# A planner that knows that two vector engines take turns, and that picks the engine itself

## Chip, cores and metric

The kernel runs on 1 core of one Trainium2 chip. The metric is device time in microseconds (us) of one execution; lower is better. The kernel before was run three times: 959.18, 959.60 and 962.43 us, median 959.6. TensorE (PE) multiplies matrices, VectorE (DVE) and GpSimd (POOL) do arithmetic on tiles, ScalarE (ACT) copies, rounds and applies functions, and SyncE (SP) issues the DMAs. SBUF is the working memory, PSUM the memory that matmuls write, in 8 banks.

## What is computed

```python
x = attention(q, k, v)      # 4 batches, 8 heads, 576 tokens, head size 64; 4 heads local, 4 strided
x = x / sqrt(mean(x*x) + 1e-6) * rms_g          # 2304 tokens x 512
x = (silu(x @ w_gate) * (x @ w_val)) @ w_out    # d_ff 1536
out = softplus(x @ w_in) @ w_out2               # d_ff 2048
```

The result is compared in float32. The weights are float64 on the host; the kernel gets their 64-bit words and decodes them to float32 on ACT and DVE.

## The kernel before

A float32 product is made of three matmuls in a reduced 32-bit format: every operand is split into a high half `h` (an ACT copy that rounds) and a low half `l = x - h` (a two-tile subtraction), and h·h, h·l and l·h are added in PSUM (`mm3`, L343 is the matmul). So each operand tile costs one ACT copy and one subtraction: `split_op` for the activations (tiles `ob`, `tb`), `part` in `prep_in` for the first weights (`win`), `prep_out` for the second weights (`wout`), `halves` for the hidden activations (`gh`/`gl`, `ghx`/`glx`).

The work runs in three stages, each recorded first and then emitted. Stage 1 is attention for batches 0 and 1. Stage 2 is attention for batches 2 and 3, laid between the first gated layer's products for tokens 0 to 1023 (`side_a`). Stage 3 holds the rest: the end of that half, `combine` and `build` (sums and differences of activation blocks for a seven-product block multiplication, `quad`), the gated layer for tokens 1024 to 2303 (f = 0 to 11), and the second layer for both halves (p = 0 to 7 twice). `out1` and `out2` multiply by the second weights; their results are added from a PSUM bank into `xs` on DVE (L771 for `out1`, L789 for `out2`), and the bank is free for the next product only after that. `plus` (L690) adds a PSUM bank to a tile in the same way, and L738 multiplies gate and value.

No instruction is placed by hand. Every step goes through `Program.add`, with its engine, an assumed duration, and the tiles that it reads and writes. `Program.emit` then plays the work through: it takes the engine that can start earliest, and of that engine's ready instructions the one with the smallest due time, counted back from the fixed order of the matmuls. The order of starts so found is the order in which each engine's instructions are issued. Engines take their instructions strictly in that order on the chip. Before, each step has a fixed engine, named in the code, and all engines are assumed to run independently. The function `two` (a two-tile sum, difference or product) goes to DVE or POOL as its caller says, with an assumed 110 + n/0.96 ns on DVE and 110 + 2.5n ns on POOL for n elements per partition:

```python
    def two(eng, n, name, o, x, y, r, w):
        if eng == "DVE":
            dve(n, lambda: getattr(nc.vector, name)(o, x, y), r, w)
        else:
            pool(n, lambda: getattr(nc.gpsimd, name)(o, x, y), r, w)
```

In the trace L263 is this operation on DVE and L265 the same on POOL. L280, L282 and L285 are the three DVE steps of `decode`. L361 to L364 are `stats` (1/rms), whose matmul with ones is L357.

Of the kernel before, what the change touches and what calls it, by code (L numbers as in the profile page):

```python
# [46 lines left out]
HOP = {"PE": 210, "DVE": 135, "ACT": 150, "POOL": 90, "SP": 60}  # L47


class Program:  # L50

    def __init__(self):
        self.nodes, self.seen, self.ends = [], {}, []
        self.free = dict.fromkeys(HOP, 0.0)
        self.side = False
        self.landed = 0.0

    def add(self, eng, dur, fn, r=(), w=(), kb=0):
        i = len(self.nodes)
        deps = set()
        for (key, lo, hi), wr in [(x, False) for x in r] + [(x, True) for x in w]:
            old = self.seen.setdefault(key, [])
            keep = []
            for e in old:
                if e[0] < hi and lo < e[1]:
                    if wr or e[3]:
                        deps.add(e[2])  # L70
                    if wr and lo <= e[0] and e[1] <= hi:
                        continue
                keep.append(e)
            keep.append((lo, hi, i, wr))
            self.seen[key] = keep
        deps.discard(i)
        self.nodes.append((eng, dur, fn, deps, 5 * kb, self.side))

    def emit(self, start=5000):
        nodes, n0, n = self.nodes, len(self.ends), len(self.nodes)  # L80
        new = range(n0, n)
        succ = {i: [] for i in new}
        left = dict.fromkeys(new, 0)
        ready = dict.fromkeys(new, 0.0)
        begin = {}

        def hop(d, i):
            e = nodes[d][0]
            return 0 if e == "PE" == nodes[i][0] else HOP[e]

        for i in new:
            for d in nodes[i][3]:
                if d < n0:
                    ready[i] = max(ready[i], self.ends[d] + hop(d, i))
                else:
                    left[i] += 1
                    succ[d].append(i)
        due = {}
        t = max(start, self.free["PE"])
        for i in new:  # L100
            due[i] = 1e12
            if nodes[i][0] == "PE":
                due[i] = t
                t += nodes[i][1]
        for i in reversed(new):
            for j in succ[i]:
                due[i] = min(due[i], due[j] - nodes[i][1] - nodes[i][4] * 2 - HOP[nodes[i][0]])
        streams = [[i for i in new if nodes[i][0] == "PE" and nodes[i][5] == s] for s in (False, True)]
        heads = [0, 0]
        free = self.free  # L110
        wait = {e: [] for e in HOP}
        avail = {e: [] for e in HOP}

        def release(i):
            if nodes[i][0] != "PE":
                heapq.heappush(wait[nodes[i][0]], (ready[i], i))

        for i in new:
            if not left[i]:
                release(i)  # L120
        ends = {}
        while len(ends) < len(new):
            best = None
            for e in HOP:
                at, s = None, 0
                if e == "PE":
                    for x in (0, 1):
                        if heads[x] < len(streams[x]) and not left[streams[x][heads[x]]]:
                            b = max(free[e], ready[streams[x][heads[x]]])
                            if at is None or b < at:  # L130
                                at, s = b, x
                elif avail[e]:
                    at = free[e]
                elif wait[e]:
                    at = max(free[e], wait[e][0][0])
                if at is not None and (best is None or at < best[0]):
                    best = (at, e, s)
            at, e, s = best
            if e == "PE":
                i = streams[s][heads[s]]  # L140
                heads[s] += 1
            else:
                while wait[e] and wait[e][0][0] <= at:
                    _, i = heapq.heappop(wait[e])
                    heapq.heappush(avail[e], (due[i], i))
                _, i = heapq.heappop(avail[e])
            begin[i] = at
            free[e] = at + nodes[i][1]
            ends[i] = free[e]
            if e == "SP":  # L150
                self.landed = max(self.landed, at + 400) + nodes[i][4]
                ends[i] = self.landed + 1100
            for j in succ[i]:
                ready[j] = max(ready[j], ends[i] + hop(i, j))
                left[j] -= 1
                if not left[j]:
                    release(j)
        for i in sorted(new, key=lambda i: (begin[i], i)):
            nodes[i][2]()
        self.ends += [ends[i] for i in new]  # L160
# [3 lines left out]
def attn_glu_softplus(  # L164
# [27 lines left out]
    def pool(n, fn, r, w):  # L192
        pr.add("POOL", 110 + n * 2.5, fn, r, w)

    def dma(kb, fn, r, w):
        pr.add("SP", 650, fn, r, w, kb=kb)
# [62 lines left out]
        sub(eng, n, l, src, h.bitcast(F32), [ksrc, kh], [kl])  # L259

    def two(eng, n, name, o, x, y, r, w):
        if eng == "DVE":
            dve(n, lambda: getattr(nc.vector, name)(o, x, y), r, w)  # L263
        else:
            pool(n, lambda: getattr(nc.gpsimd, name)(o, x, y), r, w)  # L265

    def sub(eng, n, o, x, y, r, w):
        two(eng, n, "tensor_sub", o, x, y, r, w)
# [557 lines left out]
    def w_at(f, side):  # L826
        return (f % 2, 0) if side else (0, f % 2 * 4)
# [12 lines left out]
    def prep2(p, all4, eng):  # L840
        i = ((W1N + p) % 2, 0)
        o = 3 * W1N + 4 * p
        prep_in(i, [(o, None), (o + 2, None)], True, all4, eng)
        for j in (0, 1):
            prep_out((2 * p + j) % 4, o + 2 * j + 1, None)
        return i

    with tc.manual_schedule():
# [140 lines left out]
        for side, (c0, c1, c4) in enumerate(SIDES):  # L989
# [3 lines left out]
            for p in range(n2):  # L993
                i = prep2(p, c4 is not None, "POOL" if p == 0 or side == 0 and p < 4 else "DVE")
# [85 lines left out]
```

## Time and profile before

| | |
|---|---|
| runs, median (lowest to highest) | 959.6 us (959.18 to 962.43) |
| the profiled execution | 961.84 us |
| its span, first to last instruction | 959.9 us |
| mean granted TensorE clock | 0.987 |
| PE busy | 906.0 us (94%) |
| DVE busy | 725.6 us (76%), 1184 instructions |
| ACT busy | 488.9 us (51%) |
| POOL busy | 229.8 us (24%), 201 instructions |

Busy is time in which an instruction of the engine was in execution. Two neighbours on DVE may overlap a little at their ends; the overlap counts once. The granted clock is the share of TensorE's full speed that was granted: 1.00 is 2.4 GHz, 0.5 is 1.2 GHz.

### The profile page before, as it was taken

The page shows a single profiled execution, that of the slowest core. Times are in us where ns is not written, and L with a number is a line of the kernel's source. Part 1 is how long each engine was busy: PE and PEld are TensorE (multiplying, and loading weights), DVE is VectorE, ACT ScalarE, POOL GpSimd, SP SyncE. Part 2 cuts the span into 40 slices and gives each one's busy share as a digit, 9 for nine tenths or more (in the row PEclk, how much of TensorE's full clock was granted, in tenths as well). Part 3 has the DMA queues.
Part 4 walks back from the last instruction along what each step waited for, and adds up shares of the span by engine and source line. Part 5 has one row for each costly group of instructions (what it writes and reads, how often), then busy time and mean ns, then how long its engine had stood idle before and what let it go on. Part 6 is the DMA issues. An engine that isn't in the chain of part 4 may idle for free.

```text
span 959.9 us, 14020 instructions
## 1 busy us (share of the span) xinstructions
PE 906.0 (94%) x5244; PEld 742.4 (77%) x5244; DVE 725.6 (76%) x1184; ACT 488.9 (51%) x917; POOL 229.8 (24%) x201
## 2 busy tenths in 40 slices
PE   6877999999997899999999988999989999999998
PEld 5655778778876788888788766888877888888886
DVE  6688778899389885889887796687689647666654
ACT  4677665646355465544444546655454564443331
POOL 2463102232048452324223372100023000000000
PEclk9999999999999899999999998999999999999999
DMA  9937676743140442344453013531211411101002
GB/s 193 212 116 205 178 240 176 227 149 130 66 132 22 143 118 91 99 132 145 163 174 100 23 44 100 163 89 56 76 33 39 138 43 35 44 26 42 22 1 110
DMA packets 42035, 103.11 MB, mean 107 GB/s; under 512 B 5040, under 2 KB 5744, under 8 KB 41968
## 3 DMA queue, kind: packets, MB, share of 16 engines
q1 hardware_dynamic: 41968, 102.23, 35.9%
q8 instruction: 41, 0.67, 0.3%
q14 instruction: 26, 0.21, 0.1%
HBM read 79.66 MB, written 22.54 MB: 106 GB/s over the span
## 4 chain that ended last, share of the span: by engine, by line
PE 70%; DVE 19%; DMA 4%; issue 3%; ACT 3%; POOL 1%; SPq 0%; DVEq 0%; ACTq 0%
PE bank L343 65%; DVE w L263 3%; PE bank L451 2%; DVE xs L771 2%; DVE cvu L282 2%; PE bank L532 2%; DVE cvu L280 1%; PE bank L508 1%; DMA w<-w_kept 1%; DMA id_sb<-ident 1%; DVE xs L263 1%; DVE wout L263 1%; DVE win L263 1%; DVE tb L263 1%; DVE gv L690 1%
## 5 line engine op out<-in xcount | busy, mean ns | idle before, releaser
L343 PE MATMUL bank<-ob,win 128*128 128x512 f32 (+1 forms) x1560 | 336.9, 362 | 12.0 <-ACT ob L258 3.8
L343 PEld LDWEIGHTS bank<-ob,win 128*128 128x128 f32 x1560 | 265.2, 190 | 64.2 <-ACT win L314 4.6
L343 PE MATMUL bank<-tb,win 128*128 128x512 f32 x672 | 175.5, 397 | 12.0 <-ACT ssq L686 5.5
L343 PEld LDWEIGHTS bank<-tb,win 128*128 128x128 f32 x672 | 125.9, 191 | 41.7 <-ACT ssq L686 7.4
L314 ACT ACTIVATE win<-w 128x512 fp32r<-128x512 f32 (+1 forms) x136 | 82.8, 615 | 92.2 <-DVE w L263 34.6
L789 DVE TENSOR_TENSOR xs<-bank,xs 128x512 f32<-128x512 f32 x126 | 86.7, 689 | 49.2 <-PE bank L343 48.6
L263 DVE TENSOR_TENSOR win<-w,win 128x512 fp32r<-128x512 f32 x102 | 72.7, 714 | 29.1 <-ACT win L314 28.8
L343 PE MATMUL bank<-wout,ghx 128*128 128x512 f32 x304 | 94.1, 391 | 0.4 <-DVE xs L789 0.3
L343 PE MATMUL bank<-gh,wout 128*128 128x512 f32 (+1 forms) x256 | 83.1, 361 | 7.4 <-DVE xs L771 5.9
L343 PE MATMUL bank<-ghx,wout 128*128 128x512 f32 x224 | 86.2, 404 | 0.2 <-DVE xs L771 0.2
L265 POOL TENSOR_TENSOR win<-w,win 128x512 fp32r<-128x512 f32 x34 | 49.2, 1449 | 155.1 <-ACT win L314 143.5
L343 PE MATMUL bank<-wout,gh 128*128 128x512 f32 x272 | 83.8, 390 | 0.0
L771 DVE TENSOR_TENSOR xs<-bank,xs 128x512 f32<-128x512 f32 (+1 forms) x100 | 62.2, 630 | 15.0 <-PE bank L343 14.2
L263 DVE TENSOR_TENSOR w<-w 128x256 f32<-128x256 f32 x112 | 71.9, 642 | 1.4
L343 PEld LDWEIGHTS bank<-wout,ghx 128*128 128x128 f32 x304 | 56.6, 188 | 12.9 <-DVE xs L789 1.6
L343 PEld LDWEIGHTS bank<-gh,wout 128*128 128x128 f32 x256 | 46.4, 192 | 16.9 <-DVE xs L771 7.9
L343 PE MATMUL bank<-wout,glx 128*128 128x512 f32 x152 | 59.3, 390 | 0.3 <-DVE glx L263 0.3
L343 PEld LDWEIGHTS bank<-wout,gh 128*128 128x128 f32 x272 | 50.9, 188 | 10.5
L343 PE MATMUL bank<-wout,gl 128*128 128x512 f32 x136 | 52.9, 389 | 0.0
L282 DVE SCALAR_TENSOR_TENSOR cvu<-raw,cvu 128x512 uint32<-128x512 uint32 x68 | 51.7, 760 | 1.4
L265 POOL TENSOR_TENSOR gl<-ssq,gh 128x256 fp32r<-128x256 f32 (+1 forms) x21 | 22.3, 1064 | 120.1 <-ACT gh L726 120.1
L726 ACT ACTIVATE gh<-ssq 128x512 fp32r<-128x512 f32 (+1 forms) x41 | 23.0, 564 | 54.2 <-PE bank L343 37.1
(157 smaller groups left out, 1412.8 us busy)
## 6 DMA issues: line engine op xcount, KB each, us to landing
raw<-w SPq DMA_DIRECT2D x68, 512.0 KB, 4.2
w<-w_kept SPq DMA_DIRECT2D x56, 256.0 KB, 2.7
w_kept<-cvtx SPq DMA_DIRECT2D x26, 256.0 KB, 4.2
cvt<-w_kept SPq DMA_DIRECT2D x26, 256.0 KB, 3.0
w_kept<-w SPq DMA_DIRECT2D x24, 256.0 KB, 3.9
w_kept<-cvt SPq DMA_DIRECT2D x18, 256.0 KB, 3.8
cvtx<-w_kept SPq DMA_DIRECT2D x18, 256.0 KB, 2.7
out<-xs SPq DMA_DIRECT2D x18, 256.0 KB, 2.0
```

Of the source, the lines that this page charges most:

```text
L263: dve(n, lambda: getattr(nc.vector, name)(o, x, y), r, w)
L265: pool(n, lambda: getattr(nc.gpsimd, name)(o, x, y), r, w)
L280: dve(512, lambda: nc.vector.tensor_scalar(out=u, in0=t.bitcast(U32), scalar1=0x80000000, scalar2=None, op0=ALU.bitwise_and), [kt], [ku], ...
L282: dve(512, lambda: nc.vector.scalar_tensor_tensor(out=u, in0=wlo, scalar=29, in1=u, op0=ALU.logical_shift_right, op1=ALU.bitwise_or), [kra ...
L314: act(n, lambda: nc.scalar.activation(h, t, AF.Copy), [kt], [reg(0, o + lo, o + hi)])
L343: lambda a=a, b=b, i=i, st=st, mv=mv: nc.tensor.matmul(o, lhsT=st[a], rhs=mv[b], start=(first and i == 0), stop=(last and i == m - 1), ski ...
L451: pr.add("PE", 108 if loc else 81, lambda a=a, h=h: nc.tensor.matmul(sp[64 * h:64 * h + 64, a * nk:(a + 1) * nk], lhsT=qt[:, h, q0 + a * s ...
L508: pr.add("PE", 109, lambda a=a, a0=a0, tp=tp: nc.tensor.transpose(tp[:kp, a * 128:a * 128 + 128], pv[:, a0 + a, :], id_sb), [kpv, all_of(" ...
L532: pr.add("PE", 81, lambda a=a, h=h, o=o, t=t: nc.tensor.matmul(xb[64 * h:64 * h + 64, a * nq:(a + 1) * nq], lhsT=vt[r0:r1, v0 + a, 64 * h: ...
L726: act(n, lambda: nc.scalar.activation(h, src, AF.Copy), [ksrc], [kh])
L771: dve(n, lambda: nc.vector.tensor_add(x, pb, x), [kp, kx], [kx])
L789: dve(DM, lambda: nc.vector.tensor_add(x, pb, x), [kp, kx], [kx])
```

## The change

It changes the planner and `two`, and no tile, matmul or transfer.

First, a step is marked as one that uses the port when it is on DVE or POOL and none of its tiles is a PSUM bank. The planner lets such steps run only one at a time, whichever of the two engines they are on (`self.port`). DVE has two queues for this: `DVE0` for steps with a bank, which start whenever DVE is free, and `DVE1` for the others.

Second, `two` ignores the engine that its caller names. The step is recorded for DVE with an alternative for POOL. In planning it stands in the queues `DVE1` and `FLEX`; POOL takes it from `FLEX` only if DVE has 900 ns or more of bank work before it (`BESIDE`). Its assumed durations become 60 + n/0.96 ns on DVE and 110 + 2.3n ns on POOL.

```diff
+BESIDE = 900
...
+        port = eng in ("DVE", "POOL") and not any("bank" in x[0] for x in [*r, *w])
...
+            return ("DVE1", "FLEX") if alt else (f"DVE{int(nodes[i][6])}",)
...
+            t0, t1 = earliest("DVE0", free["DVE"]), earliest("DVE1", max(free["DVE"], self.port))
...
+            base = max(free["POOL"], self.port)
+            t = earliest("FLEX", base)
+            if t is not None:
+                beside = max(0, free["DVE"] - t) + sum(nodes[i][1] for _, i in avail["DVE0"])
+                if beside >= BESIDE:
+                    offer(t, "POOL", "FLEX")
+            offer(earliest("POOL", base), "POOL", "POOL")
...
+                if s == "FLEX":
+                    nodes[i] = ("POOL", nodes[i][7][0], nodes[i][7][1]) + nodes[i][3:]
...
+            if nodes[i][6]:
+                self.port = free[e]
...
     def two(eng, n, name, o, x, y, r, w):
-        if eng == "DVE":
-            dve(n, lambda: getattr(nc.vector, name)(o, x, y), r, w)
-        else:
-            pool(n, lambda: getattr(nc.gpsimd, name)(o, x, y), r, w)
+        pr.add("DVE", 60 + n / 0.96, lambda: getattr(nc.vector, name)(o, x, y), r, w,
+               alt=(110 + n * 2.3, lambda: getattr(nc.gpsimd, name)(o, x, y)))
```

Counted over the whole program, 118 steps of `two` go from POOL to DVE and 7 the other way, so DVE has 111 instructions more and POOL 111 fewer. 2 of the 118 are in stage 1, 6 in stage 2 and 110 in stage 3. POOL keeps what attention gives it, and 9 steps of `two`. In stage 3 the matmuls stand in the same order as before.

The lines move by 39 or 40: before's L263 is L303 after (L304 on POOL), L771 is L810, L738 is L777, L690 is L729, L343 is L382, L357 is L396.

DVE, early in stage 3, while the last `out1` of tokens 0 to 1023 runs beside `combine` and `build` (win: first weights, wout: second weights, w32: weights being prepared; the last row before is the addition at 311.45 us in the trace). Before:

```order
L263 TENSOR_TENSOR ssq_65<-xs_64 128x512
L771 TENSOR_TENSOR xs_64<-bank3_74,xs_64 128x512
L263 TENSOR_TENSOR w32_83<-w32_83 128x256
L263 TENSOR_TENSOR gv0_84<-xs_64,ssq_65 128x512
L263 TENSOR_TENSOR tb_2521<-ssq_65,tb_2521 128x512
L263 TENSOR_TENSOR ob_67<-xs_64,ob_67 128x512 x2
L263 TENSOR_TENSOR tb_2521<-gv0_84,tb_2521 128x512
L263 TENSOR_TENSOR wout0_91<-cvt0_81,wout0_91 128x512
L263 TENSOR_TENSOR wout1_860<-cvtx_869,wout1_860 128x512
L738 TENSOR_TENSOR ssq_65<-bank6_77,ssq_65 128x512
L771 TENSOR_TENSOR xs_64<-bank4_75,xs_64 128x512
```

Now, from the same first row to the same last row:

```order
L303 TENSOR_TENSOR ssq_65<-xs_64 128x512
L303 TENSOR_TENSOR w32_83<-w32_83 128x256
L303 TENSOR_TENSOR ob_67<-xs_64,ob_67 128x512
L303 TENSOR_TENSOR tb_2521<-gv0_84,tb_2521 128x512
L303 TENSOR_TENSOR w32_83<-w32_83 128x256
L303 TENSOR_TENSOR tb_2521<-ssq_65,tb_2521 128x512
L303 TENSOR_TENSOR gv0_84<-xs_64,ssq_65 128x512
L303 TENSOR_TENSOR w32_83<-w32_83 128x256
L777 TENSOR_TENSOR ssq_65<-bank6_77,ssq_65 128x512
L303 TENSOR_TENSOR win0_90<-w32_83,win0_90 128x512
L303 TENSOR_TENSOR ob_67<-xs_64,ob_67 128x512
L810 TENSOR_TENSOR xs_64<-bank4_75,xs_64 128x512
```

The two `wout` subtractions and two of the `ob` and `tb` ones now stand behind the addition from the bank; a `win` subtraction that was POOL's stands ahead of it.

DVE, at the end of the gated layer, where `build` makes the operands of the second layer. Before:

```order
L690 TENSOR_TENSOR gv0_84<-bank3_74,gv0_84 128x512
L263 TENSOR_TENSOR w32_83<-w32_83 128x256
L280 TENSOR_SCALAR cvu0_82<-cvt0_81 128x512
L263 TENSOR_TENSOR w32_83<-w32_83 128x256
L282 SCALAR_TENSOR_TENSOR cvu0_82<-raw0_79,cvu0_82 128x512
L738 TENSOR_TENSOR gv0_84<-gv1_85,gv0_84 128x512
L263 TENSOR_TENSOR ssq_65<-xs_64 128x512
L771 TENSOR_TENSOR xs_64<-bank4_75,xs_64 128x512
L263 TENSOR_TENSOR w32_83<-w32_83 128x256
L285 SCALAR_TENSOR_TENSOR cvt0_81<-cvt0_81,cvu0_82 128x512
L771 TENSOR_TENSOR xs_64<-bank5_76,xs_64 128x512
```

Now:

```order
L729 TENSOR_TENSOR gv0_84<-bank3_74,gv0_84 128x512
L303 TENSOR_TENSOR ob_67<-xs_64,ob_67 128x512
L303 TENSOR_TENSOR gl1_89<-ssq_65,gh1_87 128x512
L303 TENSOR_TENSOR ob_67<-xs_64,ob_67 128x512
L777 TENSOR_TENSOR gv0_84<-gv1_85,gv0_84 128x512
L810 TENSOR_TENSOR xs_64<-bank4_75,xs_64 128x512
L303 TENSOR_TENSOR ssq_65<-xs_64 128x512
L810 TENSOR_TENSOR xs_64<-bank5_76,xs_64 128x512
L303 TENSOR_TENSOR glx0_866<-gv0_84,ghx0_863 128x512
```

The preparation of later weights (`w32`, `cvu`, `cvt`) has gone back, and the low halves `gl` and `glx`, which were POOL's, stand among the additions.

PE, from the end of stage 1 into stage 2. L532 (L571 after) is attention's last product, L343 (L382) the first gated layer's, L357 (L396) the matmul of `stats` for tokens 512 to 1023. Before:

```order
L532 MATMUL bank5_76<-pt2_117,vb1_106 64x54 x6
L532 MATMUL bank5_76<-pt3_118,vb1_106 64x54 x4
L343 MATMUL bank7_78<-ob_67,win0_90 128x512 x3
L343 MATMUL bank6_77<-ob_67,win0_90 128x512 x12
L357 MATMUL bank2_73<-ssq_65,ones_61 128x512
L343 MATMUL bank0_71<-ob_67,win0_90 128x512 x12
```

Now:

```order
L382 MATMUL bank7_78<-ob_67,win0_90 128x512 x12
L382 MATMUL bank6_77<-ob_67,win0_90 128x512 x6
L571 MATMUL bank5_76<-pt2_117,vb1_106 64x54 x6
L571 MATMUL bank5_76<-pt3_118,vb1_106 64x54 x4
L382 MATMUL bank6_77<-ob_67,win0_90 128x512 x6
L382 MATMUL bank0_71<-ob_67,win0_90 128x512 x12
L396 MATMUL bank2_73<-ssq_65,ones_61 128x512
```

The `stats` matmul now stands behind the 12 matmuls of bank0. The first 9 matmuls of bank7, which were spread among attention's before, now stand together near its end.

## Rows read from the trace of the kernel before

**Rows 1.** The page: busy time, share of the span and instructions by engine.

```profile
PE 906.0 (94%) x5244; PEld 742.4 (77%) x5244; DVE 725.6 (76%) x1184; ACT 488.9 (51%) x917; POOL 229.8 (24%) x201
```

**Rows 2.** Busy time by stretch: length, PE, PEld, DVE, ACT, POOL, clock, DMA share, GB/s.

```profile
276.00:325.00 49.00, 41.02 (x166) 31.80 (x165) 48.28 (x59) 23.85 (x45) 37.02 (x27) 0.95 0.22 68
325.00:345.00 20.00, 19.53 (x99) 16.56 (x98) 15.50 (x22) 11.02 (x21) 7.30 (x6) 0.94 0.44 138
345.00:545.00 200.00, 195.83 (x1025) 167.15 (x1024) 159.86 (x242) 95.91 (x176) 63.71 (x50) 1.00 0.39 124
545.00:600.00 55.00, 47.07 (x196) 36.63 (x195) 46.00 (x66) 30.73 (x56) 26.48 (x19) 0.91 0.21 63
...
705.00:740.00 35.00, 30.54 (x128) 23.38 (x127) 34.60 (x47) 20.39 (x37) 15.73 (x10) 1.00 0.11 31
```

**Rows 3.** Two DVE groups by form: count | busy us, mean ns of one.

```profile
L263 DVE TENSOR_TENSOR w<-w 128x256 f32<-128x256 f32 x112 | 71.9, 642 | 1.4
L263 DVE TENSOR_TENSOR gl<-raw,gh 128x256 fp32r<-128x256 f32 x16 | 6.8, 425 | 6.7 <-ACT gh L726 6.5
```

**Rows 4.** DVE's timeline at four places: start, length (us), instruction, [idle before].

```profile
278.22 1.01 DVE L361 SCALAR_TENSOR_TENSOR gv<-bank,ssq_b 128x256 f32<-128x256 f32 x2
...
299.85 0.68 DVE L263 TENSOR_TENSOR ob<-xs,ob 128x512 fp32r<-128x512 f32 x1
300.44 0.68 DVE L771 TENSOR_TENSOR xs<-bank,xs 128x512 f32<-128x512 f32 x1
301.05 1.52 DVE L263 TENSOR_TENSOR ssq<-xs 128x512 f32<-128x512 f32 x1
...
549.51 0.68 DVE L690 TENSOR_TENSOR gv<-bank,gv 128x512 f32<-128x512 f32 x1
...
707.05 0.69 DVE L690 TENSOR_TENSOR gv<-bank,gv 128x512 f32<-128x512 f32 x1 [0.34 <-PE bank L343]
...
715.93 1.77 DVE L263 TENSOR_TENSOR xs<-xs 128x512 f32<-128x512 f32 x1
```

**Rows 5.** POOL's timeline beside the second of these four places.

```profile
300.73 1.29 POOL L265 TENSOR_TENSOR glx<-gv,ghx 128x512 fp32r<-128x512 f32 x1 [0.82 <-ACT ghx L726]
301.97 1.75 POOL L265 TENSOR_TENSOR tb<-xs,tb 128x512 fp32r<-128x512 f32 x1
```

**Rows 6.** PE's timeline, 276 to 325 us: its waits.

```profile
312.18 0.50 PE L343 MATMUL bank<-gh,wout 128*128 128x512 f32 x1 [3.75 <-DVE xs L771]
...
323.60 2.75 PE L343 MATMUL bank<-tb,win 128*128 128x512 f32 x6 [2.23 <-DVE xs L771]
```

**Rows 7.** PE's timeline, 545 to 600 us: its waits.

```profile
552.19 0.54 PE L343 MATMUL bank<-gl,wout 128*128 128x512 f32 x1 [1.72 <-POOL gl L265]
566.19 0.39 PE L343 MATMUL bank<-gh,wout 128*128 128x256 f32 x1 [0.73 <-DVE xs L771]
...
579.17 2.39 PE L343 MATMUL bank<-tb,win 128*128 128x512 f32 x6 [3.17 <-ACT ssq L686]
582.24 2.93 PE L343 MATMUL bank<-tb,win 128*128 128x512 f32 x6 [0.69 <-ACT ssq L686]
```

**Rows 8.** PE's timeline, 705 to 740 us: its waits.

```profile
716.11 1.65 PE L343 MATMUL bank<-tb,win 128*128 128x512 f32 x6 [0.94 <-ACT ssq L686]
719.42 1.66 PE L343 MATMUL bank<-tb,win 128*128 128x512 f32 x6 [1.67 <-ACT gv L686]
722.57 1.66 PE L343 MATMUL bank<-ob,win 128*128 128x512 f32 x6 [1.49 <-DVE gv L690]
```

**Rows 9.** PE's timeline, 60 to 105 us: its three longest waits; and one ACT copy.

```profile
72.68 3.29 PE L343 MATMUL bank<-ob,win 128*128 128x512 f32 x12 [1.89 <-ACT win L314]
77.42 3.30 PE L343 MATMUL bank<-ob,win 128*128 128x512 f32 x12 [1.44 <-ACT win L314]
83.31 0.50 PE L343 MATMUL bank<-ob,win 128*128 128x512 f32 x1 [2.60 <-ACT ob L258]
...
84.33 0.70 ACT L394 ACTIVATE ksb<-pat 64x594 f32<-64x594 f32 x1
```

More of the change, by code (lines that the diff above doesn't have):

```diff
@@ L59, in __init__, with add @@
         self.landed = 0.0
-    def add(self, eng, dur, fn, r=(), w=(), kb=0):
+        self.port = 0.0
+    def add(self, eng, dur, fn, r=(), w=(), kb=0, alt=None):
         i = len(self.nodes)
+        port = eng in ("DVE", "POOL") and not any("bank" in x[0] for x in [*r, *w])
         deps = set()
@@ L76, in add @@
         deps.discard(i)
-        self.nodes.append((eng, dur, fn, deps, 5 * kb, self.side))
+        self.nodes.append((eng, dur, fn, deps, 5 * kb, self.side, port, alt))
     def emit(self, start=5000):
@@ L110, in emit, with queues, earliest, take @@
         free = self.free
-        wait = {e: [] for e in HOP}
-        avail = {e: [] for e in HOP}
+        wait = {q: [] for q in ("ACT", "SP", "POOL", "DVE0", "DVE1", "FLEX")}
+        avail = {q: [] for q in wait}
+        def queues(i):
+            e, alt = nodes[i][0], nodes[i][7]
+            if e != "DVE":
+                return (e,)
+            return ("DVE1", "FLEX") if alt else (f"DVE{int(nodes[i][6])}",)
         def release(i):
             if nodes[i][0] != "PE":
-                heapq.heappush(wait[nodes[i][0]], (ready[i], i))
+                for q in queues(i):
+                    heapq.heappush(wait[q], (ready[i], i))
+        def earliest(q, base):
+            for h in (wait[q], avail[q]):
+                while h and h[0][1] in begin:
+                    heapq.heappop(h)
+            if avail[q]:
+                return base
+            return max(base, wait[q][0][0]) if wait[q] else None
+        def take(q, at):
+            while wait[q] and wait[q][0][0] <= at:
+                _, i = heapq.heappop(wait[q])
+                if i not in begin:
+                    heapq.heappush(avail[q], (due[i], i))
+            while avail[q][0][1] in begin:
+                heapq.heappop(avail[q])
+            return avail[q][0]
         for i in new:
@@ L123, in emit, with offer @@
             best = None
[L124 to L135, printed above, removed]
+            def offer(at, e, s=0):
+                nonlocal best
                 if at is not None and (best is None or at < best[0]):
                     best = (at, e, s)
+            for x in (0, 1):
+                if heads[x] < len(streams[x]) and not left[streams[x][heads[x]]]:
+                    offer(max(free["PE"], ready[streams[x][heads[x]]]), "PE", x)
+            offer(earliest("ACT", free["ACT"]), "ACT", "ACT")
+            offer(earliest("SP", free["SP"]), "SP", "SP")
+            t0, t1 = earliest("DVE0", free["DVE"]), earliest("DVE1", max(free["DVE"], self.port))
+            if t0 is not None and t1 is not None and t0 == t1:
+                offer(t0, "DVE", "DVE0" if take("DVE0", t0) < take("DVE1", t1) else "DVE1")
+            else:
+                offer(t0, "DVE", "DVE0")
+                offer(t1, "DVE", "DVE1")
+            base = max(free["POOL"], self.port)
[5 more added lines that the diff above has]
+            offer(earliest("POOL", base), "POOL", "POOL")
             at, e, s = best
@@ L142, in emit @@
             else:
[L143 to L146, printed above, removed]
+                _, i = take(s, at)
+                heapq.heappop(avail[s])
+                if s == "FLEX":
+                    nodes[i] = ("POOL", nodes[i][7][0], nodes[i][7][1]) + nodes[i][3:]
             begin[i] = at
```

## The prediction

> **What bounds the kernel now.** Begin with the page: PE is busy for 906.0 us of a 959.9 us span, DVE for 725.6, ACT for 488.9, POOL for 229.8 [rows 1]. PE sets the time, and a change that touches no matmul can win two things only: the time in which PE waits, and the time in which PE runs at less than its full clock. The profiled execution took 961.84 us, 2.24 over the median of the three runs, so the sum below is made against 961.84 and 2.24 is taken off at the end.
>
> Next, the stretches of the third stage [rows 2], where 110 of the 118 moved steps lie. PE's idle time is length less busy time: 49.00 - 41.02 = 7.98 us in 276 to 325, 0.47 in 325 to 345, 4.17 in 345 to 545, 7.93 in 545 to 600 and 4.46 in 705 to 740, in all 25.0. The granted clock fell in the same places: 0.95 of 49 us is 2.45 us lost, 0.94 of 20 us is 1.2, 0.91 of 55 us is 4.95, together 8.6. Some 34 us are at stake there. In the same rows DVE is almost never free: 48.28 of 49, 46.0 of 55, 34.60 of 35. So DVE is what PE waits for in these places, although over the whole span it is busy for only 76%.
>
> Then, why DVE is so full. The mean of the 128x256 arithmetic on w32 is 642 ns, and of the like subtraction gl<-raw it is 425 [rows 3]. In the timeline, steps with a bank last 0.68 us, and so does a subtraction without one; but the SBUF step at 301.05 lasts 1.52 [rows 4], and just then two POOL instructions run, from 300.73 and from 301.97 [rows 5]. DVE's two-tile steps without a bank grow when POOL works, and POOL's 1.29 grows to 1.75. The two engines take turns. One further thing is to be seen there [rows 4]: the steps at 299.85, 300.44 and 301.05 start 0.60 us apart, less than the 0.68 that each lasts, so a queue of DVE work advances by 0.60 per step of 512 and, as an upper bound, by its duration of 0.425 per step of 256.
>
> Last, PE's own waits: 3.75 and 2.23 us for an addition into xs [rows 6]; 1.72 for a low half made on POOL, three of about 0.7 for additions (the first stands in the rows), then 3.17 and 0.69 for an ACT copy of a bank [rows 7]; 0.94, 1.67 and 1.49 [rows 8].
>
> **The change, part by part.** It removes 118 POOL steps and adds 111 to DVE net. That costs DVE up to 0.60 each, and gives back the growth of the steps that ran beside them. I counted each stretch in the new order: all of DVE's own steps at 0.60 or, for the short ones, less, plus the steps taken over. In 276 to 325 the 58 steps of its own come to 31.6 us and the 22 of POOL's 26 that it takes over to 11.6, in all 43.2 where it was busy for 48.28. The others: 43.2 for 46.0 in 545 to 600, 149.4 for 159.86 in 345 to 545, 32.3 for 34.60 in 705 to 740 [rows 2]. DVE gets more work and needs less time for it.
>
> *276 to 325.* Take the addition that ends the 3.75 us wait. In the new order it is the 43rd step behind the first pair of `stats` steps, which starts at 278.22 and lasts 1.01 [rows 4]: 279.2 + 37 x 0.60 + 6 x 0.425 = 304.0. PE wants it 3.75 us before 312.18, at 308.4 [rows 6], so this wait goes with 4.4 us in hand. The one that ends the 2.23 us wait is the 60th: 279.2 + 49 x 0.60 + 11 x 0.425 = 313.3. PE wanted it at 321.4, and without the first wait and the clock lost behind it (2.45) at 315.2 or somewhat earlier: it goes too, with 1 to 2 us in hand. That is 5.98. The other 2.0 us of idle time there are short waits for ACT and a product on DVE; I take 0.8 of them. The clock of this stretch and the next, 2.45 + 1.2, comes back with the long waits: 10.4 in all. In 325 to 345 I take nothing more.
>
> *345 to 545.* 4.17 us in waits of 1.2 at most, half of them for DVE: 2.1 (none to all, 0 to 4.2).
>
> *545 to 600.* The low half that POOL made is now the second step behind the `plus` of 549.51: done by 549.51 + 2 x 0.60 + 0.68 = 551.4, and PE, which started at 552.19 on it, gains 0.75 of 1.72. The first of the three additions is the 16th behind: 549.51 + 16 x 0.60 + 0.68 = 559.8, where PE wanted it at 565.46: three waits of 0.71, 2.13, gone. The `plus` before the 3.17 us wait is the 33rd (29 long, 4 short): 568.6, where that wait began at 576.0. So what is late next there is ACT's copy of a fresh bank alone, as in the 0.69 us wait at 582.24, which stays [rows 7]: 2.47 gained. Together 5.35. The clock: 4.95 lost in this stretch. The waits that I leave are below 1 us, and in 705 to 740 a wait of 1.67 [rows 8] left the clock at 1.00 [rows 2], so I take all 4.95.
>
> *705 to 740.* The step at 715.93, which lasted 1.77 [rows 4], is the 14th behind the `plus` of 707.05; it ends at about 715.9 where it ended at 717.70, and ACT's copy of it 1.8 earlier. The wait of 0.94 stays, 1.67 becomes 0.7, 1.49 goes, and so does one of 0.33: 2.8.
>
> *The end of stage 1.* Here the order itself changes. The `stats` matmul goes behind 12 matmuls of bank0; 12 such took 3.29 [rows 9]. ACT gets two more copies of 0.70 in front of the ob copy that PE waits for at 83.31: 1.4. PE's waits there are 1.89, 1.44 and 2.60 [rows 9]. So the ends are 4.7 lost (both additions bare on the path) and 5.9 gained (all three waits go). Nothing tells which; with two of POOL's steps and the attention's order moved I take 1.0 lost, nearest to the copies' row, since ACT's copy is what ended the longest wait.
>
> The planner's smaller durations cost nothing on the chip. They move only the order, and that is counted above.
>
> The sum: 10.4 + 2.1 + 5.35 + 4.95 + 2.8 - 1.0 = 24.6, so 961.84 - 24.6 = 937.2 for an execution like the profiled one, and 2.24 less for the median: **935 us**.
>
> **The rivals.** *DVE becomes a serial bound, and the kernel slower.* If the queue advanced by a step's whole duration, 0.685 and 0.425, DVE would need 50.1 us for the work of 276 to 325 (48.28 now), 50.4 for that of 545 to 600 (46.0) and 37.1 for that of 705 to 740 (34.60). All three rows say that PE waits for DVE there, so 1.8 + 4.4 + 2.5 would be added, and 1.0 at the start: 961.84 + 9.7 = 971.5, a median of 969. It decides above a start distance of about 0.66. Against it stand the starts 0.60 apart [rows 4]. The Trainium skill (VectorE: DVE Perf Modes, "The DRAIN you can't avoid") has this rule: the next operation doesn't start until the pipe is empty. By it the time would be the 969 just given; the same section adds that an operation which isn't held starts earlier, and the trace, with starts 0.60 apart at 0.68 each, is on the side of that addition.
>
> *The waits pass on.* With DVE early, PE's waits could end at ACT: 3.17 and 0.69 [rows 7], 0.94 and 1.67 [rows 8] already name ACT's copies, and POOL's steps needed the same copies first. If a new wait takes half of each gain, the time is 961.84 - 12.3 - 2.24 = 947. Against it: ACT is busy for 23.85 of 49 us and 30.73 of 55 [rows 2].
>
> *It does not do what it says.* The new order could shift steps to DVE while the chip's waits hang on bank hand-offs, so that early additions free a bank that no one is ready to fill; then only the start changes, 958 to 963. Against it: the 3.75 and 2.23 us waits name the additions themselves [rows 6].
>
> **How the numbers follow.** The forecast has 0.72, the passed-on waits 0.14, no difference 0.08, the slower rival 0.06. The forecast's own range: upward the start's 4.7 lost instead of 1.0 and none of 345 to 545, 5.8, so 941; downward the start's 5.9 gained, all of 345 to 545 and half of the 2.6 us of waits that I left, 6.9 + 2.1 + 1.3 = 10.3, so 925. To hold 8 in 10 it must take in most of the passed-on case, 947, with the start's bound on top of it: 925 to 951. Runs agree within about 0.5%, which is about what a measurement of this kernel can tell from no change. Over 0.5% faster (below 954.8): 0.72 + 0.14 = 0.86; within: 0.08; slower: 0.06.
>
> **What would show it.** In the profile after, POOL's busy time falls from 229.8 to about 75 and its count to 90; DVE holds 1295 instructions in about 710 us, less than before. The w32 mean falls from 642 to near 425. The waits of 3.75 and 2.23, and the three of 0.7, are gone, and the 3.17 is below 1; the clock is at 1.00 from 345 on and in what was 276 to 325. Wrong would be: the same waits, now ended by ACT copies (the second rival); DVE's total near 800, with starts 0.68 apart (the first); or a loss at 60 to 105 us of more than 5 us.

## The result and the profile after

The changed kernel takes 928.29 us, median of 4 runs (927.24 to 929.73), against 960.15 for the kernel before on the same chip: a ratio of 0.9666, 95% interval 0.9643 to 0.9689. That is 31.9 us faster, where 24.6 were forecast, to 935; 928.29 lies in the stated range of 925 to 951. The profiled execution took 928.81, its span 927.0.

The page of the kernel after, busy time by engine, beside [rows 1]:

```profile
PE 893.4 (96%) x5244; PEld 740.5 (80%) x5244; DVE 712.7 (77%) x1295; ACT 490.4 (53%) x917; POOL 77.4 (8%) x90
```

DVE holds 111 instructions more and is busy for 12.9 us less. POOL kept 11 two-tile steps; the part ahead of the prediction has 9, which was a miscount.

Two DVE groups of the kernel after, by form (count, busy us, mean ns), which answer to [rows 3]:

```profile
L303 DVE TENSOR_TENSOR w<-w 128x256 f32<-128x256 f32 x110 | 46.2, 420 | 1.1
...
L303 DVE TENSOR_TENSOR gl<-raw,gh 128x256 fp32r<-128x256 f32 x16 | 6.8, 425 | 6.6 <-ACT gh L765 6.5
```

The w32 arithmetic went from 642 ns to 420, the value of its undisturbed neighbour.

DVE's timeline of the kernel after, about where the addition at 300.44 stood before [rows 4] (start us, length us):

```profile
286.12 1.78 DVE L303 TENSOR_TENSOR gv<-xs 128x512 f32<-128x512 f32 x1
...
290.83 0.68 DVE L303 TENSOR_TENSOR tb<-gv,tb 128x512 fp32r<-128x512 f32 x1
291.44 0.68 DVE L303 TENSOR_TENSOR xs<-xs,ssq_b 128x512 f32<-128x512 f32 x1
292.04 0.68 DVE L303 TENSOR_TENSOR tb<-ssq,tb 128x512 fp32r<-128x512 f32 x1
292.64 0.68 DVE L810 TENSOR_TENSOR xs<-bank,xs 128x512 f32<-128x512 f32 x1
```

Step after step starts 0.60 us behind the last one and lasts 0.68. The one at 286.12 grew to 1.78: one of POOL's last 11 steps, a low half of 1.55 us from 285.80, ran beside it. The addition that PE waits for at 314.41 is the last of three, and ends at 312.48 + 1.87 = 314.35:

```profile
312.48 1.87 DVE L810 TENSOR_TENSOR xs<-bank,xs 128x512 f32<-128x512 f32 x3
```

Busy time by stretch in the kernel after, columns as in [rows 2] (the same times, so more work per stretch):

```profile
40.00:106.00 66.00, 52.55 (x439) 38.90 (x440) 53.67 (x101) 44.22 (x94) 25.81 (x31) 0.84 0.61 168
...
276.00:325.00 49.00, 47.99 (x223) 39.77 (x222) 48.82 (x87) 27.28 (x51) 4.59 (x4) 1.00 0.22 67
325.00:345.00 20.00, 20.00 (x107) 17.24 (x106) 19.48 (x39) 13.07 (x25) 0.00 (x0) 1.00 0.48 157
345.00:545.00 200.00, 199.02 (x1046) 171.35 (x1045) 167.52 (x307) 102.88 (x184) 2.68 (x2) 1.00 0.39 123
545.00:600.00 55.00, 53.47 (x240) 43.60 (x240) 50.03 (x94) 37.69 (x70) 1.16 (x2) 1.00 0.46 148
```

From 276 to 325 us PE does 223 matmuls where it did 166, and the clock is 1.00 from 276 on. DVE is as full as before there, with 87 steps in place of 59. The first row, 40 to 106 us, has no counterpart in [rows 2]; it reads so in the trace before, and in that of e10, a run below whose first two stages are those of before:

```profile
40.00:106.00 66.00, 50.83 (x449) 35.88 (x450) 53.88 (x100) 46.50 (x99) 30.96 (x34) 0.95 0.63 180
```

```profile
40.00:106.00 66.00, 55.04 (x449) 40.16 (x450) 53.84 (x98) 45.41 (x96) 29.94 (x34) 0.84 0.61 174
```

PE's timeline of the kernel after: its waits where [rows 6 to 9] had theirs, and one undisturbed pair:

```profile
84.13 0.49 PE L382 MATMUL bank<-ob,win 128*128 128x512 f32 x1 [3.56 <-ACT ob L299]
...
306.21 0.39 PE L382 MATMUL bank<-ghx,wout 128*128 128x512 f32 x1
306.44 0.39 PE L382 MATMUL bank<-gh,wout 128*128 128x512 f32 x1
...
314.41 1.67 PE L382 MATMUL bank<-tb,win 128*128 128x512 f32 x6 [1.01 <-DVE xs L810]
...
533.53 0.50 PE L382 MATMUL bank<-gl,wout 128*128 128x512 f32 x1 [0.98 <-DVE gl L303]
...
552.98 1.67 PE L382 MATMUL bank<-tb,win 128*128 128x512 f32 x6 [0.84 <-ACT ssq L725]
555.34 1.66 PE L382 MATMUL bank<-tb,win 128*128 128x512 f32 x6 [0.69 <-ACT ssq L725]
...
687.04 1.65 PE L382 MATMUL bank<-tb,win 128*128 128x512 f32 x6 [0.69 <-ACT ssq L725]
```

The pair at 306.21 and 306.44 is the place of the 3.75 us wait: no wait is left. The 2.23 became 1.01, the 1.72 became 0.98, the three of 0.7 are gone, the 3.17 became 0.84. At the end of stage 1 the wait of 2.60 grew to 3.56.

**Where the time went.** Both programs run the same matmuls, in stage 3 in the same order. So the start of the n-th matmul can be compared between the two traces, and the difference split by the stretches of the trace before. The table does this for four traces; the numbers are worked out from the starts of the matmuls (us, minus is earlier than before):

| stretch of before | forecast | after | e1 | e2 | e5 |
|---|---|---|---|---|---|
| 0 to 106 | +1.0 | +1.60 | -0.37 | +7.15 | +1.47 |
| 106 to 276 | 0 | -0.77 | -0.77 | -0.77 | -0.77 |
| 276 to 345 | -10.4 | -12.30 | -13.66 | -2.46 | +3.78 |
| 345 to 545 | -2.1 | -6.23 | -6.06 | -6.06 | +1.01 |
| 545 to 600 | -10.3 | -11.11 | -11.41 | -2.17 | -2.58 |
| 600 to 705 | 0 | 0.00 | 0.00 | 0.00 | 0.00 |
| 705 to 740 | -2.8 | -4.09 | -4.24 | -1.47 | -4.09 |
| 740 to the end | 0 | 0.00 | 0.00 | +0.02 | +0.04 |
| sum | -24.6 | -32.9 | -36.5 | -5.8 | -1.1 |

### The profile page after: what moved, and what is told of

Read it like the earlier page. It is cut to its first block, busy times and chain, and to the rows that moved or that the text cites. A ratio compares the mean times of both kernels' runs of the same rounds, so it can differ in the third digit from the quotient of the medians.

```text
span 927.0 us, 13935 instructions
## 1 busy us (share of the span) xinstructions
PE 893.4 (96%) x5244; PEld 740.5 (80%) x5244; DVE 712.7 (77%) x1295; ACT 490.4 (53%) x917; POOL 77.4 (8%) x90
## 4 chain that ended last, share of the span: by engine, by line
PE 87%; DVE 7%; DMA 2%; ACT 2%; issue 1%; SPq 1%; DVEq 0%; ACTq 0%
PE bank L382 81%; PE bank L490 2%; PE bank L571 2%; DVE xs L303 1%; PE bank L547 1%; DMA ql<-q_t 1%; DMA vb<-v_loc 1%; DVE xs L810 1%; DVE tb L303 1%; DVE ob L303 1%; DVE win L303 0%; PE bank L396 0%; DVE gv L303 0%; DVE w L324 0%; DVE gv L402 0%
## 5 line engine op out<-in xcount | busy, mean ns | idle before, releaser
L382 PE MATMUL bank<-ob,win 128*128 128x512 f32 (+1 forms) x1560 | 335.9, 361 | 7.6 <-ACT ob L299 3.6
L382 PEld LDWEIGHTS bank<-ob,win 128*128 128x128 f32 x1560 | 265.5, 190 | 57.6 <-ACT ob L299 4.0
L382 PE MATMUL bank<-tb,win 128*128 128x512 f32 x672 | 171.8, 391 | 3.9 <-ACT ssq L725 2.2
L382 PEld LDWEIGHTS bank<-tb,win 128*128 128x128 f32 x672 | 124.6, 188 | 31.1 <-ACT ssq L725 3.5
L303 DVE TENSOR_TENSOR win<-w,win 128x512 fp32r<-128x512 f32 (+1 forms) x135 | 91.6, 680 | 16.9 <-ACT win L353 16.7
L382 PE MATMUL bank<-wout,ghx 128*128 128x512 f32 x304 | 93.7, 389 | 0.0
L382 PE MATMUL bank<-ghx,wout 128*128 128x512 f32 x224 | 84.8, 398 | 0.0
L382 PE MATMUL bank<-wout,gh 128*128 128x512 f32 x272 | 83.8, 389 | 0.0
L382 PE MATMUL bank<-gh,wout 128*128 128x512 f32 (+1 forms) x256 | 80.2, 352 | 0.0
L810 DVE TENSOR_TENSOR xs<-bank,xs 128x512 f32<-128x512 f32 (+1 forms) x100 | 63.1, 633 | 21.5 <-PE bank L382 20.4
L382 PEld LDWEIGHTS bank<-wout,ghx 128*128 128x128 f32 x304 | 56.8, 188 | 11.6
L382 PE MATMUL bank<-wout,glx 128*128 128x512 f32 x152 | 59.2, 390 | 0.3 <-DVE glx L303 0.3
L382 PEld LDWEIGHTS bank<-wout,gh 128*128 128x128 f32 x272 | 50.9, 188 | 10.4
L382 PE MATMUL bank<-wout,gl 128*128 128x512 f32 x136 | 52.9, 389 | 0.0
L382 PEld LDWEIGHTS bank<-gh,wout 128*128 128x128 f32 x256 | 45.5, 189 | 6.5 <-ACT gh L765 0.3
L382 PEld LDWEIGHTS bank<-ghx,wout 128*128 128x128 f32 x224 | 42.1, 188 | 9.0 <-issue 0.2
L321 DVE SCALAR_TENSOR_TENSOR cvu<-raw,cvu 128x512 uint32<-128x512 uint32 x68 | 47.9, 704 | 1.2
L303 DVE TENSOR_TENSOR w<-w 128x256 f32<-128x256 f32 x110 | 46.2, 420 | 1.1
L382 PE MATMUL bank<-gl,wout 128*128 128x512 f32 (+1 forms) x128 | 45.0, 351 | 1.0 <-DVE gl L303 1.0
```

The costliest lines, as they stand in the source:

```text
L303: pr.add("DVE", 60 + n / 0.96, lambda: getattr(nc.vector, name)(o, x, y), r, w, alt=(110 + n * 2.3, lambda: getattr(nc.gpsimd, name)(o, x, ...
L321: dve(512, lambda: nc.vector.scalar_tensor_tensor(out=u, in0=wlo, scalar=29, in1=u, op0=ALU.logical_shift_right, op1=ALU.bitwise_or), [kra ...
L382: lambda a=a, b=b, i=i, st=st, mv=mv: nc.tensor.matmul(o, lhsT=st[a], rhs=mv[b], start=(first and i == 0), stop=(last and i == m - 1), ski ...
L810: dve(n, lambda: nc.vector.tensor_add(x, pb, x), [kp, kx], [kx])
```

## The experiments

The change does two things at once: it moves two-tile steps off POOL, and it gives the planner the rule that SBUF-only steps take turns. Theory E says that the engine is what pays, rival P that the order is. Every ratio is to the kernel before on the same chip.

**e1: the engine alone.** The planner of before, untouched; in its function `two`:

```diff
-        if eng == "DVE":
-            dve(n, lambda: getattr(nc.vector, name)(o, x, y), r, w)
-        else:
-            pool(n, lambda: getattr(nc.gpsimd, name)(o, x, y), r, w)
+        dve(n, lambda: getattr(nc.vector, name)(o, x, y), r, w)
```

> The planner of before, with its durations and without any notion of turns; only the engine of the two-tile steps changes: all 122 that were POOL's go to DVE. Theory E (the gain comes from the engine: with nothing on POOL beside DVE's SBUF steps these no longer grow): 925 to 936 us, the mean of the 128x256 w32 steps near 0.42 us, the waits of 3.75, 2.23 and 3.17 us gone or below 1. Rival P (the gain comes from the order that the planner finds once it knows of the turns): above 945 us, with the long waits still there.

Measured: 925.17 us, ratio 0.9636 (0.9621 to 0.9650). The page, one group and PE's waits from 545 to 555 us, from the trace of e1:

```profile
PE 893.3 (97%) x5244; PEld 739.7 (80%) x5244; DVE 717.8 (78%) x1306; ACT 491.6 (53%) x917; POOL 64.5 (7%) x79
```

```profile
L262 DVE TENSOR_TENSOR w<-w 128x256 f32<-128x256 f32 x112 | 46.8, 418 | 0.9
```

```profile
549.70 1.65 PE L340 MATMUL bank<-tb,win 128*128 128x512 f32 x6 [0.75 <-ACT ssq L683]
552.04 1.65 PE L340 MATMUL bank<-tb,win 128*128 128x512 f32 x6 [0.69 <-ACT ssq L683]
```

Theory E holds: one line in the place of four, without any rule of turns, gives the whole gain and some more. The 3.17 us wait is 0.75 here, and the 1.01 of after at 314 us is absent.

**e2: the rule alone.** The planner of after, with each step on the engine that its caller names:

```diff
-        pr.add("DVE", 60 + n / 0.96, lambda: getattr(nc.vector, name)(o, x, y), r, w,
-               alt=(110 + n * 2.3, lambda: getattr(nc.gpsimd, name)(o, x, y)))
+        if eng == "DVE":
+            pr.add("DVE", 60 + n / 0.96, lambda: getattr(nc.vector, name)(o, x, y), r, w)
+        else:
+            pr.add("POOL", 110 + n * 2.3, lambda: getattr(nc.gpsimd, name)(o, x, y), r, w)
```

> The other half: the planner of after, which lets SBUF-only steps of DVE and POOL run one at a time, with its durations, but each two-tile step on the engine that the caller names, as in before (122 on POOL). Theory E: 948 to 962 us, POOL busy about 230 us, the w32 mean above 0.55 us, since the order of issue doesn't keep the two engines apart on the chip. Rival P: 928 to 940 us.

Measured: 955.73 us, ratio 0.9956 (0.9941 to 0.9971), where theory E put it; only the w32 mean came out at 526 ns, a little under the 0.55 us expected. PE's three longest waits in the trace of e2, of those from 60 us on:

```profile
88.03 0.79 PE L384 MATMUL bank<-ob,win 128*128 128x512 f32 x1 [5.62 <-ACT ob L299]
...
330.28 0.45 PE L384 MATMUL bank<-ob,win 128*128 128x256 f32 x1 [4.40 <-ACT ob L299]
...
550.28 0.50 PE L384 MATMUL bank<-gl,wout 128*128 128x512 f32 x1 [2.16 <-POOL gl L306]
```

The rule is not worthless: it wins 12.1 us from 276 us on (the table), among them all of the 6 in 345 to 545. But 7.15 us are lost at the start, and PE still waits 2.16 us for a low half from POOL. The parts don't add up, since both cure the same waits: in 345 to 545 either alone gives 6.06.

**e5: POOL's work with nobody waiting for it.** After, with every engine's order kept, and on POOL, behind each DVE step that the caller had named for POOL in stage 3, a subtraction on a dead tile, one that no other step reads:

```diff
+        def both():
+            getattr(nc.vector, name)(o, x, y)
+            if junk and eng == "POOL":
+                j = pat[:, :min(n, 352)]
+                nc.gpsimd.tensor_sub(j, j, j)
-        pr.add("DVE", 60 + n / 0.96, lambda: getattr(nc.vector, name)(o, x, y), r, w,
+        pr.add("DVE", 60 + n / 0.96, both, r, w,
...
+        junk.append(pat)
+        nc.gpsimd.memset(pat, 0.0)
```

> After, with the order of every engine kept, and POOL given 110 subtractions of 128x352 or 128x256 on a dead tile in stage 3, one behind each two-tile step that the caller had named for POOL. Nothing reads them and they wait for nothing, so they run in a burst from about 275 us on, some 100 us of it. Theory C (DVE's SBUF steps grow only because POOL runs beside them, and PE pays where DVE is full): 940 to 965 us; the DVE steps of 276 to 345 us grow to 1.0 us and more, and PE's waits for DVE come back there, and not behind 400 us. Rival (a POOL that nobody waits for costs nothing, the growth had another cause): 926 to 931 us.

Measured: 962.37 us, ratio 1.001 (0.9992 to 1.0028). The whole gain is gone, by work that no step reads. POOL's timeline in the trace of e5: the longest runs of the added subtractions.

```profile
288.15 15.99 POOL L308 TENSOR_TENSOR pat<-pat 128x352 f32<-128x352 f32 x14
...
319.14 29.16 POOL L308 TENSOR_TENSOR pat<-pat 128x352 f32<-128x352 f32 x28
...
410.35 41.77 POOL L308 TENSOR_TENSOR pat<-pat 128x352 f32<-128x352 f32 x40
...
576.68 20.18 POOL L308 TENSOR_TENSOR pat<-pat 128x352 f32<-128x352 f32 x20
```

DVE's timeline in the trace of e5, beside the first of them; it is the stretch shown of after above:

```profile
291.87 1.26 DVE L305 TENSOR_TENSOR ssq<-xs 128x512 f32<-128x512 f32 x1
293.05 1.26 DVE L305 TENSOR_TENSOR tb<-gv,tb 128x512 fp32r<-128x512 f32 x1
294.23 1.25 DVE L305 TENSOR_TENSOR xs<-xs,ssq_b 128x512 f32<-128x512 f32 x1
295.41 1.25 DVE L305 TENSOR_TENSOR tb<-ssq,tb 128x512 fp32r<-128x512 f32 x1
296.59 0.68 DVE L816 TENSOR_TENSOR xs<-bank,xs 128x512 f32<-128x512 f32 x1
```

And three of PE's waits in the trace of e5:

```profile
310.89 0.50 PE L388 MATMUL bank<-gh,wout 128*128 128x512 f32 x1 [1.85 <-DVE xs L816]
...
334.18 2.67 PE L388 MATMUL bank<-tb,win 128*128 128x512 f32 x6 [3.38 <-ACT gv L731]
...
589.68 2.25 PE L388 MATMUL bank<-tb,win 128*128 128x512 f32 x6 [2.11 <-DVE ssq L735]
```

The same `tb` subtraction lasts 1.26 here and 0.68 in after, and the next one starts 1.18 later and not 0.60; the addition with a bank keeps its 0.68. So this is the growth by itself. Against after PE loses 16.1 us in 276 to 345, 7.2 in 345 to 545 and 8.5 in 545 to 600 (the table's differences), and nothing in 705 to 740, where POOL has run out. That the total comes back to just the time of before is chance: the added work, its amount and its places are not those of before's POOL. One thing was expected wrongly: POOL's own 11 steps stand in the same queue and hold the noise back, so it came in bursts up to 597 us and the loss with it, not before 400 alone. The Trainium skill (GPSIMD Engine Reference, "1. Specifications") says that GpSimd shares its SBUF interfaces with VectorE, with contention for VectorE instructions that are in a 2-port perf mode or have two SBUF inputs. For two SBUF inputs the traces agree: `tb` 1.26 against 0.68, the addition from a bank 0.68 in both. No row names such a mode; but a step of `decode` with a single SBUF input grew too, in the mean of all its runs from 422 ns in after (first line) to 497 in e5 (second):

```profile
L319 DVE TENSOR_SCALAR cvu<-cvtx 128x512 uint32<-128x512 uint32 x26 | 11.0, 422 | 6.5 <-ACT cvtx L318 6.4
```

```profile
L325 DVE TENSOR_SCALAR cvu<-cvtx 128x512 uint32<-128x512 uint32 x26 | 12.9, 497 | 6.0 <-ACT cvtx L324 5.8
```

**e4 and e3: the threshold.** After with `BESIDE` = 0 (e4: POOL takes a step whenever it could start it earlier) and with `BESIDE` = 1000000 (e3: never).

> After, with the threshold at 0: POOL takes a two-tile step whenever it could start it earlier than DVE, 173 steps in all, more than in before, though planned in turns. Theory E: 942 to 965 us, the w32 mean above 0.55 us, waits for DVE and for POOL's low halves back in 270 to 345 and 530 to 580 us. Rival P (POOL's steps are harmless when the planner knows that they take turns): 926 to 934 us.

> After, with a threshold that is never reached: the last 11 two-tile steps of POOL go to DVE as well. Theory E: 925 to 931 us, no difference to after outside 0.4%, since only 11 steps move. Rival P, where POOL's share beside bank work is worth something: 932 us or more, with new waits for DVE where POOL's steps stood.

Measured: e4 932.86 us, ratio 0.9713 (0.9695 to 0.9730); e3 928.22, ratio 0.9673 (0.9645 to 0.9701). For e3 the expectation of theory E holds: no difference to after. For e4 it falls, the time is the rival's. The page of e4:

```profile
PE 892.8 (96%) x5244; PEld 740.2 (79%) x5244; DVE 671.5 (72%) x1133; ACT 489.3 (53%) x917; POOL 271.1 (29%) x252
```

POOL is busier than in before (271.1 against 229.8) and the kernel is still 27 us faster. What differs is how much DVE's steps grew. Taken over 340 to 540 us as each step's length less the lower quartile of its form (the length that a quarter of its like stay under), DVE grew by 31.8 us in before while POOL was busy for 66.9, and by 11.9 in e4 while POOL was busy for 66.8. The planner lays POOL's steps beside bank work: in the same 200 us of the two traces POOL ran beside DVE's steps without a bank for 44.4 us in before and 24.1 in e4, and beside steps with a bank for 14.5 and 30.0. And it picks them: a step goes to POOL only where DVE would start it later. So "POOL beside DVE costs" is too coarse: what costs is POOL beside SBUF steps where DVE is full. e2, with the same rule but no choice of engine, shows that the choice is needed. But the choice only makes POOL's share cheap: e4 is still 4.6 us slower than e3, which leaves POOL none of these steps, and no run here shows a gain from leaving it some.

**e9: one stretch alone.** The planner of before; only the two-tile steps that are recorded between the start of stage 3 and the end of `build` go to DVE (24 of 122).

```diff
-        if eng == "DVE":
+        if eng == "DVE" or pr.move:
...
         wc = ctx.enter_context(tc.tile_pool(name="wc", bufs=1))
+        pr.move = True
...
         build(*SIDES[1], False)
+        pr.move = False
```

> Planner of before; only the 24 two-tile steps that POOL had between the start of stage 3 and the end of build, ahead of the seven-product loop, go to DVE. Theory E, where each stretch pays for its own crowding: the waits of 3.75 and 2.23 us of 276 to 325 go with the slow clock behind them, 11 to 14 us, and those behind 345 us stay: 945 to 949 us. Rival (what is saved early is lost again at the next full stretch, or the other way round): outside 942 to 953 us.

Measured: 950.98 us, ratio 0.9892 (0.9874 to 0.9909). The stretch 276 to 345 gives 11.3 us, as expected, and 1.95 are lost again in 345 to 545, for a reason that was not traced, so the time is 2 us above theory E's range, and still inside the 942 to 953 outside which the rival put it. PE's two waits and the busy time by stretch, from the trace of e9, at the place of [rows 7]:

```profile
543.33 0.50 PE L344 MATMUL bank<-gl,wout 128*128 128x512 f32 x1 [1.73 <-POOL gl L266]
...
570.28 1.66 PE L344 MATMUL bank<-tb,win 128*128 128x512 f32 x6 [3.17 <-ACT ssq L687]
```

```profile
545.00:600.00 55.00, 47.87 (x213) 37.71 (x213) 44.26 (x67) 34.56 (x63) 23.96 (x17) 1.00 0.34 106
```

The waits of 1.72 and 3.17 are still there, to 0.01 us, and yet the clock is 1.00 where before it was 0.91: the six matmuls behind the longer wait take 1.66 us and not 2.39.

**e10, e1 again and after again, on the chip of e9.** e10 is e9 without its last line: all 114 steps of stage 3 go to DVE, the 8 of stages 1 and 2 stay.

> Planner of before; only the 114 two-tile steps that POOL had in stage 3 go to DVE, 8 of stages 1 and 2 stay. Theory E (the whole gain is in stage 3): within 1.5 us of e1 on this chip. Rival (the 8 early steps are part of it): 3 us or more above e1, the difference ahead of 275 us.

> Run e1 (planner of before, every two-tile step on DVE) beside after on one chip. Its trace was 1.7 us shorter than after's in stage 3 (no wait of 1.0 at 313 us) and 2.0 at the start. If that is the kernel and not the chip: 924 to 926.5 us, and 2 to 4 below after. Rival (chips differ): within 1.5 us of after.

> The changed kernel itself, on the same chip as the next three: 926.5 to 929.5 us.

Measured: e10 926.02 us, ratio 0.9639 (0.9624 to 0.9655); e1 925.37, 0.9628 (0.9613 to 0.9643); after 930.21, 0.9675 (0.9661 to 0.9690), 0.7 above its expected range. So the gain is in stage 3, and e1 is faster than the changed kernel by 4.8 us, a little more than expected, with intervals that don't meet. Of that, 1.3 us lie in 276 to 345 (-13.64 against -12.37 in these traces), the rest mainly at the start: after's second trace is 3.18 us behind before at 106 us, e1's 0.45 ahead.

**e6, e7 and e8: durations and the start.** e6 is after with before's assumed durations (110 + n/0.96 and 110 + 2.5n), e8 is e1 with after's (60 + n/0.96). e7 is after with stage 1 planned by before's rules:

```diff
-        port = eng in ("DVE", "POOL") and not any("bank" in x[0] for x in [*r, *w])
+        port = self.turns and eng in ("DVE", "POOL") and not any("bank" in x[0] for x in [*r, *w])
...
+        if pr.turns:
             pr.add("DVE", 60 + n / 0.96, lambda: getattr(nc.vector, name)(o, x, y), r, w,
                    alt=(110 + n * 2.3, lambda: getattr(nc.gpsimd, name)(o, x, y)))
+        elif eng == "DVE":
+            dve(n, lambda: getattr(nc.vector, name)(o, x, y), r, w)
+        else:
+            pool(n, lambda: getattr(nc.gpsimd, name)(o, x, y), r, w)
...
             pr.emit()
+            pr.turns = True
```

> After, with the assumed durations of before for two-tile steps (110 + n/0.96 on DVE, 110 + 2.5 n on POOL): 14 steps on POOL in place of 11. If the durations only move the order a little, 926 to 931 us. Rival (the shorter duration is what gets DVE's order right, since a queue advances by 0.60 and not by 0.64 per step): 933 us or more, with waits for DVE back in stage 3.

> Run e1 (planner of before, every two-tile step on DVE) with the shorter assumed duration of after, 60 + n/0.96. If the durations don't matter: 924 to 926.5 us, like e1. Rival (they do): better than 922.5 or worse than 927 us.

> Stage 1 by the rules of before (fixed engines, no turns, its durations), everything else by after's. The matmul order is then before's in the whole program. If after's loss of 1.6 us at the start comes from the new order there: PE is level with before at 126 us (within 0.5) and the time is 925 to 927.5 us. Rival (the start varies by itself): 928 to 930 us, and the start is no closer to before's.

Measured: e6 927.87 us (ratio 0.9660, 0.9631 to 0.9689), e8 926.36 (0.9642, 0.9613 to 0.9671), e7 928.30 (0.9670, 0.9636 to 0.9703). The durations don't matter, as expected of both. e7 is inconclusive: in its trace the start is level with before (+0.19 at 106 us), as expected, but its runs are no faster than after's, on another chip. The traces lean one way: at 106 us the seven with the new rules in stage 1 (after twice and e2 to e6) are 1.2 to 7.2 us behind before, and the six that plan it as before does (e1 twice and e7 to e10) lie within 0.7 of before. What the start's order costs in the time of a run is open within some 2 us.

## Why the prediction was right, and where it was off

*DVE is what PE waits for, and its own steps are stretched by POOL.* Right, and shown: e5 brings the stretching back without moving a step, and the gain is gone; e1 takes it away without the rule, and gives all the gain.

*DVE needs less time for more work.* Right: 712.7 us with 1295 instructions, where about 710 was said; POOL 77.4 where 75 was said; w32 at 420 ns where 425 was.

*276 to 345, 10.4 forecast, 12.3 measured.* The 3.75 us wait went, as worked out. The 2.23 did not quite: its addition was to end at 313.3 and did so at about 314.35, and PE was there at 313.40, earlier than the 315.2 allowed for. The growth of 1.1 us at 286.12, beside a step that POOL kept, is as much as the addition is late; in e1 and e3, with no such step, this wait is absent. That it was more than forecast all the same comes from the short waits, of which 0.8 us were counted: all went, and by the starts of the matmuls they were worth over 3, 0.6 of it in 325 to 345, where nothing was taken.

*345 to 545, 2.1 forecast, 6.2 measured.* This is the term that was most mis-sized, and 4.1 of the 8.3 us by which the sum over the traces fell short. The step that failed is "half of them for DVE". Two of PE's waits there, from the trace before:

```profile
470.48 1.67 PE L343 MATMUL bank<-tb,win 128*128 128x512 f32 x6 [1.19 <-DVE gv L690]
...
478.62 1.66 PE L343 MATMUL bank<-tb,win 128*128 128x512 f32 x6 [0.91 <-ACT gv L686]
```

By the row the second is a wait for ACT's copy of a bank. But that copy stood on ACT behind an instruction that waited 2.98 us for an addition on DVE, and the addition behind grown steps, the last of 1.78. ACT, then DVE, in the trace before:

```profile
477.45 0.63 ACT L737 ACTIVATE ssq<-ssq 128x512 f32<-128x512 f32 x1 [2.98 <-DVE ssq L690]
477.99 0.58 ACT L686 ACTIVATE gv<-bank 128x512 f32<-128x512 f32 x1
```

```profile
475.04 1.78 DVE L285 SCALAR_TENSOR_TENSOR cvtx<-cvtx,cvu 128x512 uint32<-128x512 uint32 x1
476.74 0.68 DVE L690 TENSOR_TENSOR ssq<-bank,ssq 128x512 f32<-128x512 f32 x1
```

So that wait was DVE's at one remove, and so was the other one put down to ACT, 0.67 at 414.60, behind a wait of 1.99 for DVE. In after no wait of either kind is left in this work. And the idle time of PE, 4.17 us, understates the waits, since each is counted from the modelled end of the matmul before it. The wait of 1.19 us holds the next matmul back by 1.35 (starts 1.57 apart instead of 0.23), the 3.75 by 3.91.

*545 to 600, 10.3 forecast, 11.1 measured.* The parts came out as said: 0.98 is left where 0.97 was worked out, 0.84 where 0.7 was, the three of 0.7 went, and the clock is at 1.00. But e9 shows that the reason given for the clock, that the long waits bring it down, isn't the whole: the same waits left it at 1.00 there. The number was right for this execution; the cause of the fall is open.

*705 to 740, 2.8 forecast, 4.1 measured.* The wait of 0.94 was to stay and the 1.67 to leave 0.7. In after two waits of 0.69 are left, the first of them in the place of the 0.94; the rest is again mostly what idle time doesn't show.

*The start, 1.0 forecast, 1.6 measured* (3.18 in the second trace): ACT's copies did push back the ob copy, and the wait of 2.60 became 3.56. The granted clock of 40 to 106 us, 0.84 where the trace before has 0.95, differs there too, but it doesn't explain the loss: e10 has 0.84 as well, and is 0.57 us ahead of before at 106 us.

*The rivals.* The serial DVE is refuted by after's own timeline, with starts still 0.60 apart in the stretch where it is fullest. The waits passed on to ACT only where the sum had them, at 0.7 to 0.8. That the change would do nothing but move the start, at 958 to 963, is refuted by the time.

## What to carry to other kernels

Look at the spread of one operation's duration before looking at an engine's total: 642 ns against 425 for the same kind of step was the first sign of the whole case. An engine that nobody waits for can still cost time through another that is full: in e5 about a third of its added busy time. So give a second engine work that leaves the first alone, or that is picked where the first has none of the kind that suffers, and check that this gains anything at all: with these two-tile steps it did not. And when a planner's rule and a plain removal cure the same waits, test the removal by itself: here one line beat the rule by 0.5%.

## What was not expected of the hardware

POOL work of 107 us (87.8 in steps of 128x352 and 19.5 of 128x256) that nothing waits for cost 34 us: 962.37 for e5 against 928.30 on the same chip for e7, which differs from after in its first stage alone. It came through DVE's steps without a bank. Taken as for e4, each step's length less the lower quartile of its form, the steps beside POOL's grew by 43 us from 266 to 600 us: 40 of it in steps with two SBUF inputs, 3.3 in those of `decode` with one, and none in those with a bank, which last as long beside POOL as alone.

The clock: waits of 1.73 and 3.17 us left the granted clock at 1.00 in e9, and waits of 1.72 and 3.17 at the same matmuls went with 0.91 in before, where the matmuls behind them were 0.43 us apart instead of 0.23. Between the two waits PE ran the same matmuls in the same order with the same three waits of 0.7, in e9 with two more of 0.58 and 0.42. No run here tells what decides it.
